# A fused attention and two-MoE kernel whose order of work comes from a planner: new DMA and TensorE costs in the planner, another gate and rank for the first W_out, early scales for the second weights, and half-size store buffers

## The chip, the cores and the metric

One Trainium2 chip, one core. The metric is the device time of one execution in microseconds (us), as the median over runs. The engines are named as in the profile: PE is TensorE's matmul side and PEld its weight loads, DVE is VectorE, ACT is ScalarE, POOL is GpSimd, and SP is SyncE, whose queue issues nearly all DMAs here.

## The reference, cut to what matters

Causal attention with a linear memory branch, mixed by a per-head gate, feeds two feed-forward layers with different activations, one after the other, on 2304 tokens.

```python
B, H, S, D = (4, 8, 576, 64)
scores = scale * np.matmul(q, k.transpose(0, 1, 3, 2))      # causal mask, softmax -> a
local = np.matmul(a, v)
mem_out = einsum(phi(q), M_prev) / (einsum(phi(q), z_prev) + 1e-06)
x = g * mem_out + (1 - g) * local                           # -> (2304, 512)
h = x @ w_in;  x = (h * sigmoid(h)) @ w_out                 # layer 0: 512 -> 2048 -> 512
h = x @ w_in2; y = (h * tanh(softplus(h))) @ w_out2         # layer 1: the same sizes
```

## The kernel before, in words

**Order of the work.** The kernel text does not issue instructions in the order in which it stands. Each operation is handed to a `Plan` (line 58 on) with a priority, the regions that it reads and writes, its engine or choice of engines, and a cost in ns. `Plan.issue` (line 105) then plays the whole program through as a list scheduler: at each step the engine that is free first takes, among the operations that are ready by then, the one with the smallest priority number, and that fixes each engine's in-order instruction stream. An operation is ready when what it depends on has ended plus a latency `LAT` (by the engine that produced it, `LAT["SP"]` for anything that comes by DMA) plus `MORE` for some pairs of engines. A DMA ends at `max(moved, issue end + 650) + tail`, so that the planner's DMAs pass one after the other; `tail` is bytes/360 for a copy (line 416) and 112 ns for each 128x128 block of a transpose (line 594). A priority decides only between operations that are ready together: an engine with nothing better takes whatever is there, and does not break it off. On the chip each stream runs in order, so an instruction that is planned too early makes everything behind it on its engine wait.

**Stages.** Attention goes in 80 steps (16 head pairs x query blocks, two visits each; `stage_a` line 538: scores, mask, exponentials, split into two f16 parts, a DMA transpose; `stage_b`: probabilities x values and normalisation, three steps later; `stage_c`: a PE transpose into x). Its results go by DMA into `xd`, and layer 0 takes them in 9 chunks of 256 tokens. Chunk 0 needs steps 0 to 7, chunk 1 (the second chunk) steps 8 to 15, and so on. For a chunk, `chunk_x` (line 775) scales x and splits it into two f16 parts, `gemm1` computes one of 8 groups of hidden columns in 24 matmuls of 128x256 (three products of parts), `hidden` applies the activation, and `gemm2` adds 24 matmuls more into the output banks. The buffers of the hidden values are 7 deep. `flush` copies a chunk's outputs into two staging buffers `w` and stores them to `yd`. Layer 1 uses 7 products of quarter blocks in place of 8 (`gemm1`, `gemm2` with l = 1) and reads its weights in that form.

**First weights.** `weights_of(k)` (line 955) handles W_in (k = 0, units 0 to 7) and W_out (k = 1, units 8 to 15), 1 MB each. A unit is loaded (`ws<-w` or `w<-w` in the profile), turned from float64 bits into float32 by two ACT operations and one on DVE (`single`: ACT L705, ACT L348, DVE L356), and its products with itself (8 matmuls `banks<-w` into `gram`) give a bound from which `weight_scale` finds one scale for all 8 units. Only then `weight_split` makes the two f16 parts of each (an ACT copy and a DVE operation). The load of unit u waits for the single of unit u - FLIGHT, and W_out's loads wait also for the split of attention step GATE (line 1023). `W_PRIO` (line 911) gives W_in's work the priority -2e5 + u and W_out's -1e5 + u; the attention steps below 8 have -1.5e5 + 2.3 n and the others 2.3 n. Work of the MoE on ACT, DVE and POOL has -1e6 + i and so goes first; its matmuls have 1e6 + i and so go last.

**Second weights.** `weight_single` (line 737) loads each of the 16 units of layer 1 during attention, makes it single, notes its largest square sum (`squares`, into `topw`) and stores it to `wd`. When chunk 8's input is set up, `weight_scale(1, k)` finds the two scales from `topw` (`largest`, line 659: a DVE product with the identity, a small matmul `banks<-diag,onesf` into bank 7, a DVE maximum), and `weight_pair` (line 757) loads the units again, forms sums of blocks and writes two f16 parts of 1792 columns. Units 0 to 7 go into the space that attention has left, 8 to 11 into that of the first weights when these are done with, and 12 to 15 (u >= LATE) through one buffer, the second stage `wb[1]`, into `wp` in HBM, from where `weight_fetch` brings them back.

Of the kernel before, what the change touches and what calls it, by code (L numbers as in the profile page):

```python
# [41 lines left out]
G_AHEAD = 3  # L42
G_DEEP = 7
LEAD = 7
GATE = 4
FLIGHT = 4
LATE = NU - NU // 4


# [9 lines left out]
class Plan:  # L59

    LAT = {"PE": 197, "ACT": 250, "DVE": 220, "POOL": 130, "SP": 920}
    MORE = {("ACT", "POOL"): 20, ("DVE", "POOL"): 20, ("POOL", "PE"): 45, ("PE", "ACT"): 17}

    def __init__(self):
# [120 lines left out]
def attn_moe_moe2_kernel(ctx: ExitStack, tc: tile.TileContext, kq, vm, beta, w1, w2, out):  # L187
# [88 lines left out]
    def carve(shape, dt, n=1):  # L276
        ts = []
        for _ in range(n):
# [9 lines left out]
            if len(shape) > 1:  # L288
# [27 lines left out]
    b8r = ring([wb[0], wb[1], side[0], side[1], wb[0], wb[1], side[0], wb[0],  # L316
                side[0], wb[0], side[0], wb[0], side[0], wb[0], wb[1], side[0]])
    tw = w_first[:, 2048 * NU + 2048:2048 * NU + 4096].bitcast(F32)
    w_out2 = w_first[:, 0:NU // 2 * 3584].rearrange("p (u s b c) -> p u s b c", u=NU // 2, s=2, b=7)


# [54 lines left out]
    def stt(prio, out, in0, s, in1, op0, op1):  # L376
        plan.add(prio, [c_stt(out, in0, s, in1, op0, op1)], [out], aps(in0, s, in1), shared=not ps(in0) and not ps(in1))
# [17 lines left out]

    def mm(prio, ms, whole=False):

        ns, edge, before = 0, None, 0
        for o, l, r, _, _ in ms:
            n = cols(o)  # L400
            load, one, times = (107, 2 * n / 2.4 + 2.5, 2) if r.dtype == F32 else (107 if r.dtype == F32R else 14, n / 2.4 + 2.5, 1)
            for _ in range(times):
                ns += (one + (0 if edge is None else max(0, load - before))) * l.shape[0] / 128
                edge = (edge or (load, 0))[0], one
                before = one

        def go():
            for o, l, r, a, z in ms:
                nc.tensor.matmul(out=o, lhsT=l, rhs=r, start=a, stop=z)  # L409

        writes = [m[0] for m in ms]
        if whole:
            writes = [(t, 0, 128, b0 // 2048 * 2048, -(-b1 // 2048) * 2048) for t, _, _, b0, b1 in map(plan.region, writes)]
        plan.add(prio, [("PE", ns, go)], writes, [x for m in ms for x in m[1:3]], edge=edge)

    def dma(prio, out, in_, writes=None, reads=None):
        nbytes = 128 * cols(out) * SIZE[out.dtype]
        plan.add(
            prio, [("SP", 475, lambda: nc.sync.dma_start(out=out, in_=in_))],
            [out] if writes is None else writes, [in_] if reads is None else reads, tail=nbytes / 360)  # L420

    def other(prio, e, ns, fn, writes, reads=()):
        plan.add(prio, [(e, ns, fn)], writes, reads)
# [114 lines left out]
    def stage_a(n, sbk, prio):  # L538

        v, qt = STEPS[n]  # L540
        nk = qt + 1
        N = min(S, 128 * nk)
        b0 = 512 * sbk[turn[0] % len(sbk)]
        turn[0] += 1
        ph, P, m1 = phr(), pr(), mr()
        if qt < 4:

            scs = [banks[:, b0 + 512 * e:b0 + 512 * e + N] for e in range(2)]
            ms, nb = [], 4 * nk
            for e, sc in enumerate(scs):  # L550
                r, c = slice(64 * e, 64 * e + 64), slice(128 * (qt % 2), 128 * (qt % 2) + 128)
                if qt < 2:
                    ms.append([(sc, qq[v, 0][r, c], rk[v][r, 0:N], True, False)])
                else:
                    kh, kl, (qh, ql) = *kk[v], qq[v, 1]
                    ms.append([(sc, qh[r, c], kh[r, 0:N], True, False), (sc, qh[r, c], kl[r, 0:N], False, False),
                               (sc, ql[r, c], kh[r, 0:N], False, False)])
            masks = [(sc[:, N - 128:N], ident16, mask[:, 0:128], False, True) for sc in scs]
            mm(prio, [x for y in zip(*ms) for x in y] + masks)
            both = banks[:, b0:b0 + 1024].rearrange("p (e c) -> p e c", e=2)[:, :, 0:N]  # L560
            P = P[:, 0:2 * N].rearrange("p (e c) -> p e c", e=2)
            ph_ = ph[:, 0:nb].rearrange("p (s e k) c -> p s e (k c)", s=2, e=2)
            tiles = [(P[:, e], scs[e], m1[:, e:e + 1]) for e in range(2)]
        else:
            nb = 2 * nk
            both = banks[:, b0:b0 + N]
            kh, kl = kk[v]
            hi, lo = [t.rearrange("p e q -> p (e q)") for t in q4s]
            ms = []
            for a, z in ((0, 512), (512, N)):  # L570
                ms += [(both[:, a:z], hi, kh[:, a:z], True, False), (both[:, a:z], hi, kl[:, a:z], False, False),
                       (both[:, a:z], lo, kh[:, a:z], False, z < N)]
            mm(prio, ms + [(both[:, N - 64:N], ident16, mask[:, 128:192], False, True)])
            pad = P[:, N:128 * nk]
            other(prio, "POOL", 90, lambda: nc.gpsimd.memset(pad, 0.0), [pad])
            tiles = [(P[:, 0:N], both, m1[:, 0:1])]
            P = P[:, 0:128 * nk]
            ph_ = ph[:, 0:nb].rearrange("p (s k) c -> p s (k c)", s=2)
        m1 = m1[:, 0:len(tiles)]
        other(prio, "DVE", 1.04 * cols(both) + 70, lambda: nc.vector.tensor_reduce(  # L580
            out=m1, in_=both, axis=AX, op=ALU.max, negate=True), [m1], [both])
        for o, sc, m in tiles:
            act(prio, o, sc, AF.Exp, 1.0, m)
        copy(prio + D_S, ph_[:, 0], P, PSCALE)
        stt(prio + D_S, ph_[:, 1], P, PSCALE, ph_[:, 0], ALU.mult, ALU.subtract)
        plan.mark(f"step{n}")
        ph = ph[:, 0:nb]

        live = pt_live[1 - LAG:]
        p0 = next(x for x in [pt_live[-1][1], 0] + [z for _, z in live] if x + nb <= PT_BLOCKS and all(  # L590
            z <= x or x + nb <= a for a, z in live))
        pt_live.append((p0, p0 + nb))
        pt = pts[n] = pt_tile[:, p0:p0 + nb, :]
        plan.add(prio, [("SP", max(1180, 400 + 113 * nb), lambda: nc.sync.dma_start_transpose(
            out=pt, in_=ph.rearrange("p n c -> p (n c)")))], [pt], [ph], tail=112 * nb)

    def last(n):
        v, qt = STEPS[n]
# [36 lines left out]
    def stage_c(n, prio):  # L635

        if not last(n):
            return
        v, qt = STEPS[n]
        p = VISITS[v][0]  # L640
        x, R = xts.pop(n)
        m = 1 + qt % 2
        for i in range(m):
            x2, o = x[:, i].rearrange("p e d -> p (e d)"), bank[6 + i][:, 260:260 + R]
            plan.add(prio, [("PE", 56, lambda o=o, x2=x2: nc.tensor.transpose(o, x2, ident[0:R, 0:R]))], [o], [x2, ident],  # L645
                     edge=(107, 56))
        b, hp = divmod(p, H // 2)
        if b == 0 and qt < 2:
            copy(prio, xs0[:, hp].rearrange("p (b c) -> p b c", b=m),
                 banks[:, 512 * 6:512 * 8].rearrange("p (b c) -> p b c", b=2)[:, 0:m, 260:260 + R])  # L650
            return
        xo = xor_()[:, 0:m * R]
        copy(prio, xo.rearrange("p (b c) -> p b c", b=m),
             banks[:, 512 * 6:512 * 8].rearrange("p (b c) -> p b c", b=2)[:, 0:m, 260:260 + R])
        t0, n = column(b, 256 * (qt // 2)), m * R
        dma(prio, xd[128 * hp:128 * hp + 128, t0:t0 + n], xo, writes=[("xd", hp, hp + 1, t0, t0 + n)])
# [100 lines left out]
    def weight_pair(u, prio):  # L757
# [4 lines left out]
                            ("POOL", "DVE"))  # L762
        sc, v = wsc[1][:, k:k + 1], b8[:, 256:2048]
        d = (w_in2, w_out2)[k][:, j].rearrange("p s b c -> p s (b c)")
        w = wb[1].bitcast(F16)[:, 0:3584].rearrange("p (s n) -> p s n", s=2) if u >= LATE else d
        act(prio, w[:, 0], v, AF.Copy, sc)
        stt(prio, w[:, 1], v, sc, w[:, 0], ALU.mult, ALU.subtract)
        if u >= LATE:
            dma(prio, wp[u - LATE], wb[1].bitcast(F16)[:, 0:3584], writes=[("wp", u, u + 1, 0, 1)])

    def weight_fetch(u, prio):
        dma(prio, w_first[:, 3584 * (u - NU // 2):3584 * (u - NU // 2 + 1)], wp[u - LATE], reads=[("wp", u, u + 1, 0, 1)])


    def chunk_x(l, c, prio, spot):
# [132 lines left out]
    D_B, D_C, D_Q, D_K, D_P, D_V, D_S = 2.5, 3.2, 4.0, 4.0, 3.0, 6.0, 0.5  # L908
    A_RATE, MOE_B, L_V = 2.3, -1e6, 0.0
    att_prio = lambda n, d=0: A_RATE * (n + d) + (ATT_B if n < N0 else 0)  # L910
    MOE, W_PRIO, ATT_B = MOE_B, (-2e5, -1e5), -1.5e5

    def prep(v, prio):
        if VISITS[v][1][-1] >= 2:
# [66 lines left out]
    def inputs(l, c, prio):  # L981

        nonlocal n_att
        if l == 0:
# [4 lines left out]
                n_att += 1  # L989
            for u in range(NU * (c - 1) // TOPS, min(NU, NU * c // TOPS)) if c else ():  # L990
                weight_single(u, att_prio(12 + 3.5 * u))
        xs_of[l, c] = chunk_x(l, c, prio, bank[0] if (l, c) == (0, 0) else bank[7])
        if (l, c) == (0, NT // TOK - 1):
            for k in range(2):
                weight_scale(1, k, 1e5 + NU, bank[7])
            for u in (*range(NU // 2), *range(LATE, NU)):
                weight_pair(u, 1e5 + NU + u)

# [83 lines left out]
```

## Time and profile before

| | us |
|---|---|
| median of 3 runs (966.07 to 967.75) | 966.64 |
| the profiled execution | 968.1 |
| its span, first to last instruction | 966.2 |
| mean granted TensorE clock | 0.973 |
| PE busy in the span | 911.2 (94%) |
| DVE, ACT, POOL busy | 725.1, 609.4, 404.9 |
| time in which the 16 DMA engines' packets of the SP queue were moving | 51.0% |

PE's busy time is that of overlapping matmuls; what it was not busy for are gaps in which its next matmul waited for something. The granted clock is the share of TensorE's full 2.4 GHz that was granted: 0.5 is 1.2 GHz.

### The profile page before, as it was taken

What the parts mean: (1) busy time and instruction counts of PE and PEld (TensorE: products, weight loads), DVE (VectorE), ACT (ScalarE), POOL (GpSimd) and SP (SyncE); (2) the same over time, 40 slices, a digit from 0 to 9 for tenths busy, and PEclk for the clock granted to TensorE, in tenths of its full rate; (3) what the DMA queues carried; (4) which work ended last, traced back from release to release, by engine and by line L of the source; (5) the groups of instructions that cost most, each with busy time, mean ns of one, the idle gap of its engine ahead of it and who ended that gap; (6) DMA issues with size and microseconds to landing.
All of it is one profiled execution on the core that took longest, in us unless ns stands there. A gap on an engine that the chain in (4) does not pass through costs nothing.

```text
span 966.2 us, 25452 instructions
## 1 busy us (share of the span) xinstructions
PE 911.2 (94%) x10436; PEld 800.8 (83%) x10436; DVE 725.1 (75%) x1534; ACT 609.4 (63%) x1074; POOL 404.9 (42%) x573
## 2 busy tenths in 40 slices
PE   4659989899999989999998999999999999999997
PEld 3547878787878878788887888999999999999996
DVE  5797877697778878778458735757887888878775
ACT  7897888787878866666345545544645545544543
POOL 1113223233324525334334767454545635635453
PEclk9658999999999999999999999999999999999999
DMA  9987399899899896866422433320010010010010
GB/s 283 333 293 190 68 300 272 206 284 224 219 280 244 213 197 161 172 139 117 97 90 88 148 121 127 127 93 24 23 46 23 24 45 24 24 43 14 13 24 22
DMA packets 154579, 131.28 MB, mean 136 GB/s; under 512 B 111712, under 2 KB 138848, under 8 KB 150368
## 3 DMA queue, kind: packets, MB, share of 16 engines
q1 hardware_dynamic: 154320, 129.68, 51.0%
q8 instruction: 81, 1.33, 0.6%
q14 instruction: 34, 0.28, 0.1%
q10 hardware_dynamic: 144, 0.00, 0.0%
HBM read 77.75 MB, written 25.69 MB: 107 GB/s over the span
## 4 chain that ended last, share of the span: by engine, by line
PE 78%; DMA 9%; DVE 6%; ACT 4%; issue 2%; SPq 0%; POOL 0%; DVEq 0%; ACTq 0%
PE banks L409 77%; DMA arena<-vm 2%; ACT arena L348 2%; DVE w L356 1%; DMA arena<-kq 1%; DMA wp<-ws 1%; DMA w<-w 1%; DMA yd<-w 1%; PE banks L645 1%; DVE arena L356 1%; ACT w L348 1%; DVE ws L356 1%; ACT ws L348 1%; DMA ws<-w 1%; DVE arena L362 1%
## 5 line engine op out<-in xcount | busy, mean ns | idle before, releaser
L409 PEld LDWEIGHTS <-w 128*128 128x128 f16 (+1 forms) x3584 | 346.5, 100 | 68.0 <-DVE w L356 19.6
L409 PE MATMUL banks<-arena 128*128 128x128 f16 (+6 forms) x4752 | 295.6, 223 | 19.0 <-ACT arena L348 8.0
L409 PEld LDWEIGHTS <-arena 128*128 128x128 f16 (+1 forms) x4464 | 232.4, 100 | 20.6 <-issue 11.3
L409 PE MATMUL banks<-xh,w 128*128 128x256 f16 x1728 | 211.7, 273 | 4.3 <-DVE ga L356 3.3
L409 PE MATMUL banks<-g,w 128*128 128x256 f16 x1728 | 211.2, 274 | 2.2 <-ACT w L348 2.1
L409 PE MATMUL banks<-w,g 128*128 128x256 f16 x1512 | 181.1, 273 | 0.0
L409 PEld LDWEIGHTS <-g 128*128 128x128 f16 x1512 | 144.1, 98 | 15.1
L362 POOL TENSOR_TENSOR g<-ga,g 128x512 f16<-128x512 f32 x71 | 96.8, 1366 | 110.5 <-ACT g L348 105.0
L362 POOL TENSOR_TENSOR arena<-arena 128x256 f32<-128x256 f32 (+1 forms) x71 | 60.1, 852 | 125.8 <-DVE arena L362 110.5
L356 DVE SCALAR_TENSOR_TENSOR arena<-arena 128x256 f16<-128x256 f32 (+6 forms) x144 | 106.6, 748 | 7.6 <-ACT arena L348 7.4
L362 POOL TENSOR_TENSOR xh<-xh 128x128 f32<-128x128 f32 x139 | 70.9, 533 | 92.5 <-ACT xh L348 90.5
L348 ACT ACTIVATE arena<-arena 128x256 f32<-128x256 f32 (+6 forms) x179 | 101.1, 591 | 9.3 <-PE banks L409 5.2
L362 POOL TENSOR_TENSOR w<-w 128x128 f32<-128x128 f32 x140 | 79.7, 592 | 45.6 <-ACT w L348 43.5
L348 ACT ACTIVATE arena<-banks,arena 128x128 f32<-128x128 f32 (+4 forms) x144 | 73.8, 545 | 32.2 <-DVE arena L580 29.3
L356 DVE SCALAR_TENSOR_TENSOR ga<-ga,banks 128x512 f32<-128x512 f32 x72 | 49.1, 683 | 41.0 <-ACT ga L348 40.4
L348 ACT ACTIVATE ga<-banks,xsc 128x512 f32<-128x512 f32 x72 | 49.1, 684 | 40.9 <-PE banks L409 39.2
L580 DVE TENSOR_REDUCE arena<-banks 128x2 f32<-128x256 f32 (+3 forms) x80 | 64.1, 802 | 11.9 <-PE banks L409 10.1
L356 DVE SCALAR_TENSOR_TENSOR g<-w,xsc,g 128x384 f16<-128x384 f32 (+1 forms) x72 | 55.6, 776 | 15.6 <-ACT g L348 15.6
L356 DVE SCALAR_TENSOR_TENSOR g<-xh,xsc,g 128x384 f16<-128x384 f32 (+1 forms) x72 | 54.5, 759 | 15.6 <-ACT g L348 13.3
L348 ACT ACTIVATE w<-banks 128x128 f32<-128x128 f32 x72 | 19.5, 270 | 67.9 <-PE banks L409 67.9
L348 ACT ACTIVATE g<-w,xsc 128x384 f16<-128x384 f32 (+1 forms) x72 | 47.0, 660 | 19.2 <-POOL w L362 18.9
L348 ACT ACTIVATE g<-xh,xsc 128x384 f16<-128x384 f32 (+1 forms) x72 | 47.6, 663 | 16.5 <-POOL xh L362 15.0
(118 smaller groups left out, 1129.6 us busy)
## 6 DMA issues: line engine op xcount, KB each, us to landing
ws<-w SPq DMA_DIRECT2D x22, 1024.0 KB, 6.7
arena<-kq SPq DMA_DIRECT2D x16, 576.0 KB, 5.1
w<-w SPq DMA_DIRECT2D x8, 1024.0 KB, 9.4
wd<-w SPq DMA_DIRECT2D x16, 512.0 KB, 4.6
arena<-vm SPq DMA_DIRECT2D x16, 325.0 KB, 3.6
yd<-w SPq DMA_DIRECT2D x36, 128.0 KB, 2.7
ws<-wd SPq DMA_DIRECT2D x9, 512.0 KB, 3.5
xs<-yd SPq DMA_DIRECT2D x9, 512.0 KB, 3.7
```

The costliest lines, as they stand in the source:

```text
L348: return ("ACT", ns, lambda: nc.scalar.activation(out=out, in_=in_, func=func, scale=scale, bias=bias))
L356: return ("DVE", 1.04 * cols(out) + 160 - over[0], lambda: nc.vector.scalar_tensor_tensor(out=out, in0=in0, scalar=s, in1=in1, op0=op0, op ...
L362: return (e, ns, lambda: eng.tensor_tensor(out=out, in0=in0, in1=in1, op=op))
L409: nc.tensor.matmul(out=o, lhsT=l, rhs=r, start=a, stop=z)
L580: other(prio, "DVE", 1.04 * cols(both) + 70, lambda: nc.vector.tensor_reduce(out=m1, in_=both, axis=AX, op=ALU.max, negate=True), [m1], [b ...
L645: plan.add(prio, [("PE", 56, lambda o=o, x2=x2: nc.tensor.transpose(o, x2, ident[0:R, 0:R]))], [o], [x2, ident], edge=(107, 56))
```

## The change

- In the planner: `LAT["SP"]` from 920 to 1800 ns; a copy's tail from bytes/360 to bytes/315; a transpose's tail from 112 to 220 ns a block; f32 and f32r matmuls and the PE transposes of `stage_c` get other costs (the f16 matmuls keep theirs).
- GATE from 4 to 2 and FLIGHT from 4 to 3.
- W_out's priority from -1e5 + u to 20 + u, so 28 to 35; attention step 8 has 18.4, step 12 has 27.6 and step 15 has 34.5.
- `weight_scale(1, k)` is called right after the last single of each half of the second weights, with the priority -1e6, and no longer at chunk 8's input with 1e5 + 16.
- Units 12 to 15 of the second weights: three rotating buffers of one part each (`tw`, and the two halves of `wb[1]`) and two stores of 448 KB, where there was one buffer of both parts and one store of 896 KB.

```diff
-GATE = 4
-FLIGHT = 4
+GATE = 2
+FLIGHT = 3
-    LAT = {"PE": 197, "ACT": 250, "DVE": 220, "POOL": 130, "SP": 920}
+    LAT = {"PE": 197, "ACT": 250, "DVE": 220, "POOL": 130, "SP": 1800}
+    halfr = ring([tw.bitcast(F16)[:, 0:1792], *[wb[1].bitcast(F16)[:, 1792 * i:1792 * i + 1792] for i in range(2)]])
-        ns, edge, before = 0, None, 0
+        ns, edge = 0, None
         for o, l, r, _, _ in ms:
             n = cols(o)
-            load, one, times = (107, 2 * n / 2.4 + 2.5, 2) if r.dtype == F32 else (107 if r.dtype == F32R else 14, n / 2.4 + 2.5, 1)
-            for _ in range(times):
-                ns += (one + (0 if edge is None else max(0, load - before))) * l.shape[0] / 128
-                edge = (edge or (load, 0))[0], one
-                before = one
+            load, more = (107, 58) if r.dtype == F32 else (107, 42) if r.dtype == F32R else (14, 2.5)
+            one = max((2 if r.dtype == F32 else 1) * n / 2.4 * l.shape[0] / 128 + more, 30)
+            ns += one
+            edge = (edge or (load, 0))[0], one
-            [out] if writes is None else writes, [in_] if reads is None else reads, tail=nbytes / 360)
+            [out] if writes is None else writes, [in_] if reads is None else reads, tail=nbytes / 315)
-            out=pt, in_=ph.rearrange("p n c -> p (n c)")))], [pt], [ph], tail=112 * nb)
+            out=pt, in_=ph.rearrange("p n c -> p (n c)")))], [pt], [ph], tail=220 * nb)
-            plan.add(prio, [("PE", 56, lambda o=o, x2=x2: nc.tensor.transpose(o, x2, ident[0:R, 0:R]))], [o], [x2, ident],
+            plan.add(prio, [("PE", 131, lambda o=o, x2=x2: nc.tensor.transpose(o, x2, ident[0:R, 0:R]))], [o], [x2, ident],
-        w = wb[1].bitcast(F16)[:, 0:3584].rearrange("p (s n) -> p s n", s=2) if u >= LATE else d
-        act(prio, w[:, 0], v, AF.Copy, sc)
-        stt(prio, w[:, 1], v, sc, w[:, 0], ALU.mult, ALU.subtract)
+        w = [halfr() for _ in range(2)] if u >= LATE else [d[:, i] for i in range(2)]
+        act(prio, w[0], v, AF.Copy, sc)
+        stt(prio, w[1], v, sc, w[0], ALU.mult, ALU.subtract)
         if u >= LATE:
-            dma(prio, wp[u - LATE], wb[1].bitcast(F16)[:, 0:3584], writes=[("wp", u, u + 1, 0, 1)])
+            for i in range(2):
+                dma(prio, wp[u - LATE, :, 1792 * i:1792 * i + 1792], w[i], writes=[("wp", u, u + 1, i, i + 1)])
-    MOE, W_PRIO, ATT_B = MOE_B, (-2e5, -1e5), -1.5e5
+    MOE, W_PRIO, ATT_B = MOE_B, (-2e5, 20.0), -1.5e5
                 weight_single(u, att_prio(12 + 3.5 * u))
+                if u % (NU // 2) == NU // 2 - 1:
+                    weight_scale(1, u // (NU // 2), MOE, bank[7])
         if (l, c) == (0, NT // TOK - 1):
-            for k in range(2):
-                weight_scale(1, k, 1e5 + NU, bank[7])
```

## Rows read from the trace of the kernel before

**Rows 1.** Busy time by stage; after each engine's us the instructions, then clock, DMA share, GB/s.

```profile
0.00:34.00 34.00, 18.93 (x124) 12.95 (x124) 21.00 (x52) 25.63 (x48) 4.76 (x27) 0.99 0.97 312
34.00:77.36 43.36, 27.03 (x203) 20.88 (x204) 37.05 (x79) 38.48 (x59) 5.17 (x6) 0.50 0.99 295
77.36:515.00 437.64, 420.28 (x4576) 351.50 (x4575) 335.91 (x693) 316.64 (x578) 154.96 (x169) 1.00 0.80 191
515.00:966.20 451.20, 444.95 (x5537) 415.43 (x5535) 331.11 (x712) 228.62 (x391) 239.98 (x371) 1.00 0.17 54
```

**Rows 2.** Timeline of PE, around the first gemm1 and the first gemm2.

```profile
73.77 2.74 PE L409 MATMUL banks<-w 128*128 128x128 bf16 x24 [1.70 <-DVE w L356]
...
77.36 2.04 PE L409 MATMUL banks<-xh,w 128*128 128x256 f16 x15
...
99.89 0.49 PE L409 MATMUL banks<-g,w 128*128 128x256 f16 x3
...
101.07 8.02 PE L409 MATMUL banks<-g,w 128*128 128x256 f16 x72
```

**Rows 3.** Groups by line in 40 to 77.36 us: busy, mean ns, idle before.

```profile
L409 PE MATMUL banks<-w 128*128 128x128 bf16 x64 | 7.9, 309 | 6.9 <-DVE w L356 6.9
...
L705 ACT ACTIVATE w<-ws 128x1024 f32<-128x1024 f32 x4 | 4.5, 1133 | 2.5 <-DMA ws<-w 2.4
...
L705 ACT ACTIVATE w<-w 128x1024 f32<-128x1024 f32 x3 | 3.4, 1123 | 0.0
```

**Rows 4.** Timeline of DVE: the first and the last of three W_out singles.

```profile
57.18 1.22 DVE L356 SCALAR_TENSOR_TENSOR w<-w,ws 128x1024 uint32<-128x1024 uint32 x1
...
63.18 1.22 DVE L356 SCALAR_TENSOR_TENSOR w<-w 128x1024 uint32<-128x1024 uint32 x1
```

**Rows 5.** Timeline of ACT after the first gemm1: two waits, the last W_out single.

```profile
78.06 0.62 ACT L348 ACTIVATE arena<-banks,arena 128x128 f32<-128x128 f32 x2 [2.29 <-DVE arena L580]
...
81.65 0.38 ACT L348 ACTIVATE arena<-banks 128x256 f32<-128x256 f32 x1 [2.21 <-PE banks L645]
...
84.43 1.13 ACT L705 ACTIVATE w<-w 128x1024 f32<-128x1024 f32 x1
```

**Rows 6.** Timeline of SP's queue: the longest issue of a transpose.

```profile
24.51 8.43 SPq L594 DMA_TRANSPOSE arena<-arena  x1
```

**Rows 7.** DMA issues: count, KB each, median us from issue to landing.

```profile
ws<-w SPq DMA_DIRECT2D x22, 1024.0 KB, 6.7
...
yd<-w SPq DMA_DIRECT2D x36, 128.0 KB, 2.7
...
wp<-ws SPq DMA_DIRECT2D x4, 896.0 KB, 5.3
...
arena<-arena SPq DMA_TRANSPOSE x80, 5.0
```

**Rows 8.** Timeline of PE: the three gaps of over 2 us after 78 us.

```profile
220.39 0.81 PE L409 MATMUL banks<-g,w 128*128 128x256 f16 x6 [2.13 <-ACT w L348]
...
362.74 0.49 PE L409 MATMUL banks<-diag,onesf 128*128 128x128 f32 x2 [2.43 <-DVE arena L362]
...
514.64 2.01 PE L409 MATMUL banks<-xh,w 128*128 128x256 f16 x9 [2.71 <-DVE ga L356]
```

**Rows 9.** Busy time of the 20 us around each of these gaps, columns as in rows 1.

```profile
220.00:240.00 20.00, 19.53 (x208) 16.10 (x208) 14.72 (x36) 16.68 (x29) 6.19 (x8) 0.91 1.00 233
360.00:380.00 20.00, 17.52 (x185) 14.18 (x184) 17.14 (x37) 12.34 (x23) 10.51 (x12) 1.00 0.74 170
500.00:520.00 20.00, 16.89 (x139) 14.28 (x137) 17.32 (x32) 10.32 (x10) 9.03 (x6) 0.91 0.28 87
```

**Rows 10.** Chain that ended last: pieces ahead of the first two of these gaps.

```profile
213.59 5.79 DMA yd<-w
...
360.61 4.31 DMA yd<-w
```

**Rows 11.** Timeline of ACT: the first split of the second weights.

```profile
504.59 1.79 ACT L348 ACTIVATE arena<-ws,wsc 128x1792 f16<-128x1792 f32 x1 [4.82 <-DVE wsc L353]
```

More of the change, by code (lines that the diff above doesn't have):

```diff
@@ L764, in weight_pair @@
         d = (w_in2, w_out2)[k][:, j].rearrange("p s b c -> p s (b c)")
-        w = wb[1].bitcast(F16)[:, 0:3584].rearrange("p (s n) -> p s n", s=2) if u >= LATE else d
-        act(prio, w[:, 0], v, AF.Copy, sc)
-        stt(prio, w[:, 1], v, sc, w[:, 0], ALU.mult, ALU.subtract)
+        w = [halfr() for _ in range(2)] if u >= LATE else [d[:, i] for i in range(2)]
+        act(prio, w[0], v, AF.Copy, sc)
+        stt(prio, w[1], v, sc, w[0], ALU.mult, ALU.subtract)
         if u >= LATE:
-            dma(prio, wp[u - LATE], wb[1].bitcast(F16)[:, 0:3584], writes=[("wp", u, u + 1, 0, 1)])
+            for i in range(2):
+                dma(prio, wp[u - LATE, :, 1792 * i:1792 * i + 1792], w[i], writes=[("wp", u, u + 1, i, i + 1)])
     def weight_fetch(u, prio):
-        dma(prio, w_first[:, 3584 * (u - NU // 2):3584 * (u - NU // 2 + 1)], wp[u - LATE], reads=[("wp", u, u + 1, 0, 1)])
+        dma(prio, w_first[:, 3584 * (u - NU // 2):3584 * (u - NU // 2 + 1)], wp[u - LATE], reads=[("wp", u, u + 1, 0, 2)])
     def chunk_x(l, c, prio, spot):
```

## The prediction

> **What bounds the kernel now.** The first view is the busy time by stage [rows 1]. In the last stage, from 515 us on, PE is busy for 444.95 of 451.20 us, and what is missing is nearly all the end, where the last outputs are drained. Here PE is the bound and nothing of the change touches its matmuls. From 77.36 to 515 us it is busy for 420.28 of 437.64, so 17.4 us are gaps. Before 77.36 it is busy for 18.93 + 27.03 of 77.36 us: 31.4 us are gaps, and the 27.03 us of the second row ran at a granted clock of 0.50, the 1.2 GHz level. So at most some 49 us of gaps and 13.5 us of half clock are to be had, and three fifths of it lie before the first gemm1.
>
> The second view is the timeline of PE there [rows 2]. The first gemm1 begins at 77.36 us, right behind 24 W_out matmuls; the first gemm2 at 99.89, without a gap before it. From then on PE always has gemm work, so an earlier first gemm1 moves everything behind it, provided that W_out is ready when the hidden buffers are full. What holds gemm1 back is ACT and DVE, busy for 38.48 and 37.05 of 43.36 us [rows 1]. The groups by line [rows 3] tell with what: seven W_out singles stand on ACT in this stretch (4 + 3 operations of L705 of 1.13 us, each followed by a second one that I take at the same length), 7 x 2.26 = 15.8 us, though their result isn't needed before 99.89.
>
> The third view is PE's gaps one by one after 78 us [rows 8]. Three are over 2 us, 2.13 + 2.43 + 2.71 = 7.3 of the 17.4 us; the other 10.1 us are pieces below that. Around two of them the granted clock of 20 us is 0.91 in place of 1.00 [rows 9], that is 0.09 x 20 / 0.5 = 3.6 us at half clock, 1.8 us lost for each.
>
> **The change part by part.** The sum is made against the profiled execution, 968.1 us, of which 966.2 are the span and 1.9 lie around it; the median of the runs shown is 966.64, 1.5 lower, and the difference is carried over to it.
>
> *Step 1, W_out behind the second chunk's attention.* On the path to the first gemm1 W_out costs three things. ACT stood for 2.4 us in front of a W_out load that had not landed [rows 3], with W_in's and the attention's work queued behind it. On DVE three W_out singles of 1.2 us stand among the W_in splits and the normalisation of chunk 0's last step [rows 4], 3.6 us. And the 24 matmuls ahead of gemm1 took 2.74 us at half clock [rows 2]. Together 8.7 us, if all of it goes and nothing takes its place. But the planner fills a free engine with whatever is ready, and steps 8 to 11 now stand in W_out's place; their pieces are shorter, so that they hold up less. I take -5.0, between 0 and -8.7.
>
> *Step 2, what is late next: gemm2.* The singles taken off ACT there have to be made after it, in competition with `hidden` (which goes first) and steps 8 to 11. Before, PE had 22.5 us between first gemm1 and first gemm2: at 8.02/72 us a matmul [rows 2] a gemm1 of 24 is 2.7 us, eight for a chunk 21.4 us, and the rest attention. Eight can be worked off before the buffers are full. With gemm1 5 us earlier PE has work of its own until some 94 + 5 = 99 us. If W_out's last single, at 84.43 us [rows 5], moves little, this costs nothing; if all 15.8 us move behind gemm1, less the 4.5 us in which ACT now waits there [rows 5], gemm2 comes 11.3 us later, at 111, and PE stands for 12. The loads themselves aren't the limit, since GATE lets them begin two steps sooner. I take +2.5, between 0 and +14 (12 and one return to half clock of 1.8).
>
> *Step 3, three loads in flight, GATE 2.* The longest issue of a transpose took 8.43 us [rows 6], with four loads of 1 MB queued ahead of it; SP could issue nothing else, neither attention inputs nor the next load. With three queued the stall should be shorter by about one load's passage. Against it, the fourth load waits for the first single. Nothing shows the net: between -3 and +2.5; I take 0, as W_in's chain is bound by ACT and DVE after 40 us.
>
> *Step 4, the planner's costs.* Worked out for the mean transpose of 10 blocks, the old planner had 1.53 + 0.65 + 1.12 + 0.92 = 4.2 us from issue to landing and the new has 6.2; the trace shows 5.0 [rows 7]. For 128 KB it is 2.4 and 3.3 against 2.7; for 1 MB 5.0 and 6.3 against 6.7. So the old costs are short for all three and the new ones long for the first two. In an in-order queue the two errors don't cost the same: planned too early, the instruction makes all behind it wait; planned too late, other ready work goes first, and PE has some nearly always. The first two gaps of rows 8 stand behind stores to `yd` of 5.79 and 4.31 us in the chain [rows 10], twice and 1.6 times the median of 2.7 [rows 7]: a staging buffer was not free when the copy into it came up, and gemm2 waited for that copy. These two, 2.13 + 2.43 + 1.8 of clock = 6.4 us, should mostly go, and a part of the 10.1 us in pieces; but a new order brings gaps of its own. The f32 and transpose costs on PE change only when the planner thinks PE free; their matmuls are the same. I take -4.5, between -11 and +4.
>
> The Trainium skill (TensorE: Matmul & The Clock Gate, Part 1) says that the throttled clock is the default state and that activity releases it. The trace agrees around the gaps at 220 and 514 us (0.91), not at 362 us (1.00) nor in the first 34 us (0.99 with PE busy for little over half) [rows 1, 9]; by the rule the third gap would be worth 1.8 us more, -6.3 in place of -4.5.
>
> *Step 5, early scales and half buffers.* ACT waited 4.82 us for the scale and then began on splits of 1.79 us each [rows 11], and `hidden` waits for one that is under way; PE's gap of 2.71 us at 514.64 stands behind that [rows 8]. With the scale ready before chunk 8 the splits can begin some 5 us sooner and spread out: 2.7 + 1.8 of clock = 4.5 us at best. Against it, two more small `diag` matmuls stand among attention and wait on PE's queue for DVE; such a one waited 2.43 us [rows 8], with all of gemm and attention queued behind it, so up to +4.8. I take -2.0. The half buffers shorten a row of stores of 5.3 us each [rows 7] between which ACT and DVE wait for the one buffer; while it ran PE had gemm work of layer 0, so it is 0 now, and a cover only if PE comes there some 10 us earlier. Four more issues on SP and the shared `tw` cost nothing there for the same reason.
>
> Sum: -5.0 + 2.5 + 0 - 4.5 - 2.0 = -9.0, so 959.1 us in a profiled execution and **957.6 us** as a median.
>
> **The rivals.**
>
> *More comes than forecast.* Step 1 near its end (-8), gemm2 not late (0), SP's stalls shorter (-2), step 4 at -7, step 5 at -3: -20, 947 us. For it speaks that each end is a row; against it that work displaced from a full ACT has to go somewhere.
>
> *The priorities don't bite.* ACT and DVE have free moments before 77 us, a ready W_out single is taken whatever its number, and three singles on DVE were planned there although W_in's and chunk 0's work came first by priority even then. Then first gemm1 and gemm2 stay, and the reordering trades one gap for another: 966, within 2.
>
> *Slower: W_out comes too late.* All seven singles fall behind steps 8 to 12 and behind the first single of the second weights (27.6, so ahead of all of W_out; three ACT operations like L705's, 3.4 us). gemm2 then begins at 111 + 3 = 114 us against work until 99: PE stands for 15 and loses 1.8 to the clock. With -5 from step 1 and -6.5 from steps 4 and 5 that is +5.3, 972 us. It decides from where gemm2 comes more than some 11 us after PE has run dry. For it speaks that ACT is the fullest engine there; against it that ACT waited 4.5 us right after 77 us and that the same work as before is to be done by gemm2's start.
>
> **How the numbers follow.** The forecast has 0.50, more than forecast 0.20, no bite 0.10, too late 0.20. What a measurement of this kernel can tell from no change is about 0.2%, 1.9 us. Faster by more than that: the first two and little of the third, 0.72; within it 0.08; slower, the last, 0.20. The likeliest case alone lies between 951 and 964, by steps 1 and 2, of which one gives back what the other brings. Eight times in ten takes in the low rival's centre and the slower one's: 947 to 972 us.
>
> **What would show it.** In the profile after, the first gemm1 (`banks<-xh,w`) should come at 69 to 74 us and W_out's matmuls for the most part behind it; the first gemm2 (`banks<-g,w`) at 98 to 103 with a gap of at most 3 us. The transposes' issues on SP before 40 us should stay under 6 us. The three gaps over 2 us should be gone, and the stage from there to 515 us should have some 11 us of gaps, not 17.4. No wait of ACT for `wsc` should be left about 500 us, and from 520 us on the trace should read as before, earlier by the difference. A first gemm1 not earlier than 76 us, or a gap of 6 us and more before the first gemm2, makes the forecast wrong; so do new gaps of over 2 us between 100 and 500 us.

## The result, and the profile after

The changed kernel takes 953.01 us (median of 4 runs, 951.2 to 954.03) against 967.19 us of the kernel before in the same comparison: a ratio of 0.9848, 95% interval 0.9822 to 0.9874. That is 14 us faster where 9 were forecast, inside the range. The profiled execution took 952.23 us, its span is 950.1.

The first view is the busy time by stage, first of the kernel after with the stages of [rows 1].

```profile
0.00:34.00 34.00, 16.20 (x116) 10.61 (x116) 19.00 (x51) 25.29 (x48) 4.80 (x27) 0.96 0.94 267
34.00:77.36 43.36, 30.66 (x241) 23.15 (x242) 35.17 (x79) 35.18 (x60) 6.62 (x8) 0.64 0.86 247
77.36:515.00 437.64, 429.80 (x4688) 361.81 (x4687) 346.15 (x694) 329.42 (x585) 159.37 (x173) 0.99 0.81 198
515.00:950.10 435.10, 428.37 (x5395) 400.75 (x5393) 326.46 (x711) 226.50 (x385) 229.32 (x368) 1.00 0.17 57
```

The same view cut at 120 us tells more, since by then the wait for W_out is over in both kernels. After:

```profile
0.00:120.00 120.00, 85.89 (x742) 65.87 (x742) 91.53 (x206) 100.37 (x178) 26.38 (x48) 0.83 0.88 240
120.00:515.00 395.00, 390.78 (x4302) 329.69 (x4301) 308.79 (x617) 289.51 (x514) 144.41 (x159) 1.00 0.80 196
```

and before:

```profile
0.00:120.00 120.00, 88.61 (x752) 69.96 (x753) 94.65 (x206) 97.38 (x169) 23.00 (x46) 0.82 0.81 234
120.00:515.00 395.00, 377.64 (x4151) 315.36 (x4150) 299.31 (x617) 283.36 (x516) 141.89 (x156) 1.00 0.83 199
```

Up to 120 us the change wins nothing: PE is busy 2.7 us less at nearly the same clock. From 120 to 515 us its gaps fall from 17.4 to 4.2 us, and that is most of the 16.1 us by which the span is shorter.

One reading of [rows 1] has to be put right for the clock. The 0.99 of the first 34 us is not a measured level: the trace before has its first clock record at 30.05 us (after: at 24.13), and the view counts what has no record as 1.00. The matmuls show the other level there. Two sets of eight products of a weight unit, before:

```profile
15.38 1.04 PE L409 MATMUL banks<-w 128*128 128x128 bf16 x8 [4.70 <-DVE w L356]
31.38 0.63 PE L409 MATMUL banks<-w 128*128 128x128 bf16 x8
```

The first took as long as such sets at a recorded 0.50 (1.03 us at 62.05), the second as those at 1.00 (0.62 us at 89.97). So the time up to the first record is counted at 0.50 from here on, and a loss is PE's gaps plus half of the time that it was busy at 0.50. Over the whole span that is 55.0 + 25.7 = 80.7 us before and 45.1 + 20.0 = 65.0 after, 15.7 of the 16.1 us. Up to 120 us it is 53.7 and 54.1, from 120 to 515 us 19.2 and 4.2.

The start does look as drawn, and more so. The timeline of PE in the kernel after, around the first gemm1, the last W_out matmuls and the first gemm2, to be set beside [rows 2]:

```profile
64.08 0.37 PE L409 MATMUL banks<-xh,w 128*128 128x256 f16 x1 [1.59 <-ACT xh L349]
66.55 1.86 PE L409 MATMUL banks<-xh,w 128*128 128x256 f16 x8 [2.10 <-DVE xh L357]
...
95.33 3.44 PE L409 MATMUL banks<-xh,w 128*128 128x256 f16 x30
...
103.80 1.03 PE L409 MATMUL banks<-w 128*128 128x128 bf16 x8 [1.99 <-DVE w L357]
...
109.18 0.40 PE L409 MATMUL banks<-g,w 128*128 128x256 f16 x1
110.93 1.05 PE L409 MATMUL banks<-g,w 128*128 128x256 f16 x8 [1.36 <-DVE w L357]
```

The first gemm1 comes 13.3 us sooner, though PE waits again after its first matmul, until 66.55 us; the first gemm2 comes 9.3 us later. Chunk 0's gemm1s are used up at some 99 us, and for ten us PE has only attention and W_out's own products. W_out's last single, at 84.43 us before [rows 5], is on ACT at

```profile
99.45 1.14 ACT L705 ACTIVATE w<-w 128x1024 f32<-128x1024 f32 x1
```

Busy time, clock and DMA of the wait, and of the part of it at half clock:

```profile
100.00:112.00 12.00, 8.57 (x60) 5.71 (x58) 10.07 (x28) 10.04 (x21) 2.93 (x3) 0.72 1.11 228
102.64:109.46 6.82, 5.64 (x37) 3.84 (x37) 5.73 (x21) 4.90 (x12) 0.00 (x0) 0.50 1.16 281
```

3.4 us of gaps, and 5.64 us of work at half clock, which is 2.8 us more lost: together some 6 us. That is about what the early gemm1 and the clock had won by then (up to 95 us the loss is 47.6 us, before 53.7). From chunk 1's first gemm2, at 148.7 us as against 148.4 before (counted off in the trace, 192 matmuls to a chunk), both kernels stand level with their gemms; by chunk 4's the changed one is 26 us ahead (336.8, 363.2), more than all the loss of the middle, so a part of it is attention put off; at layer 1's first gemm2 it is 16.3 (617.6, 633.9).

What PE waited for from 120 to 515 us, after:

```profile
PE banks L409 <- POOL g L363: 0.9, 1, 0.9
PE banks L645 <- DVE mx L366: 0.9, 1, 0.9
```

and before:

```profile
PE banks L409 <- DVE arena L362: 5.6, 6, 2.4
PE banks L409 <- ACT arena L348: 3.4, 3, 1.6
PE banks L409 <- DVE ga L356: 3.1, 2, 2.7
PE banks L409 <- ACT w L348: 2.1, 1, 2.1
```

All three gaps of [rows 8] are gone and no group of waits is over 1 us. That is the middle; which part of the change emptied it is for the experiments.

### The profile page after: what moved, and what is told of

Read it like the earlier page. It is cut to its first block, busy times and chain, and to the rows that moved or that the text cites. A ratio compares the mean times of both kernels' runs of the same rounds, so it can differ in the third digit from the quotient of the medians.

```text
span 950.1 us, 25452 instructions
## 1 busy us (share of the span) xinstructions
PE 905.0 (95%) x10436; PEld 796.3 (84%) x10436; DVE 726.8 (76%) x1532; ACT 616.4 (65%) x1075; POOL 400.1 (42%) x574
## 4 chain that ended last, share of the span: by engine, by line
PE 55%; DVE 1%; ACT 1%; issue 1%; DMA 0%; POOL 0%; ACTq 0%; DVEq 0%
PE banks L409 55%; DVE arena L357 0%; ACT arena L349 0%; PE banks L645 0%; DVE ws L357 0%; ACT w L349 0%; DVE arena L363 0%; DMA yd<-w 0%; POOL g L363 0%; DVE diag L354 0%; DVE mx L366 0%; ACT g L349 0%; ACT ga L349 0%; DVE ga L357 0%; DVE w L357 0%
## 5 line engine op out<-in xcount | busy, mean ns | idle before, releaser
L357 DVE SCALAR_TENSOR_TENSOR arena<-arena 128x256 f16<-128x256 f32 (+6 forms) x144 | 112.5, 789 | 11.2 <-ACT arena L349 11.0
L363 POOL TENSOR_TENSOR arena<-arena 128x256 f32<-128x256 f32 x72 | 64.8, 907 | 132.7 <-DVE arena L363 113.1
L349 ACT ACTIVATE arena<-arena 128x256 f32<-128x256 f32 (+6 forms) x184 | 105.0, 593 | 20.6 <-PE banks L409 15.8
L349 ACT ACTIVATE arena<-banks,arena 128x128 f32<-128x128 f32 (+4 forms) x144 | 73.7, 546 | 32.0 <-DVE arena L580 23.8
L357 DVE SCALAR_TENSOR_TENSOR g<-w,xsc,g 128x384 f16<-128x384 f32 (+1 forms) x72 | 54.9, 770 | 17.2 <-ACT g L349 16.8
L349 ACT ACTIVATE g<-ga 128x512 f16<-128x512 f32 x72 | 45.2, 628 | 18.6 <-DVE ga L357 18.2
```

Of the source, the lines that this page charges most:

```text
L349: return ("ACT", ns, lambda: nc.scalar.activation(out=out, in_=in_, func=func, scale=scale, bias=bias))
L357: return ("DVE", 1.04 * cols(out) + 160 - over[0], lambda: nc.vector.scalar_tensor_tensor(out=out, in0=in0, scalar=s, in1=in1, op0=op0, op ...
L363: return (e, ns, lambda: eng.tensor_tensor(out=out, in0=in0, in1=in1, op=op))
```

## The experiments

All stand against the kernel before on the same chip (its medians were 972.1, 969.6 and 970.6 us in the three sets), so ratios are compared. "Costs" is LAT["SP"], the DMA tails and the f32 and transpose costs; "rank" is W_out's priority with GATE 2 and FLIGHT 3; "scales" the early scales and the half buffers. The gaps are 395 less PE's busy time from 120 to 515 us, in the one profiled execution of each kernel. The theories' times were written for 967.2 us before; a ratio of 0.99 is 957.5 us on that scale.

**Set 1: one part at a time.** Costs alone (`e1_costs`):

```diff
-    LAT = {..., "SP": 920}
+    LAT = {..., "SP": 1800}
-    tail=nbytes / 360    tail=112 * nb
+    tail=nbytes / 315    tail=220 * nb
```

with the diff's lines for f32 matmuls and `stage_c`'s transposes.

> The kernel before with the planner's new costs alone (LAT, DMA tails, f32 and transpose costs); W_out's rank, GATE, FLIGHT, scales and half buffers stay old. Theory A, the costs carry the gain: the stage from 120 to 515 us loses little, some 953 to 956 us. Theory B, the rank of W_out with GATE and FLIGHT carries it, since attention is ahead afterwards: 965 us or more. Theory C, the early scales carry a third (the gap at 514 us): about 958 us with a gap of over 2 us at chunk 8.

Measured: 0.992 (0.9892 to 0.9947), 964.1 us (959.5 on that scale, between the theories). The middle did become calmer (7.1 us of gaps, of which 4.8 from 130 to 160 us), but the second weights took 6.2 us back, and up to 120 us the loss is 55.3 us as against 53.7. Busy time of both stretches:

```profile
130.00:160.00 30.00, 25.21 (x231) 19.89 (x230) 21.94 (x52) 23.36 (x45) 7.44 (x9) 0.94 0.99 264
515.00:640.00 125.00, 118.79 (x1208) 107.24 (x1206) 83.74 (x124) 68.56 (x89) 85.15 (x80) 1.00 0.42 136
```

Rank alone (`e2_rank`):

```diff
-GATE = 4, FLIGHT = 4, W_PRIO = (-2e5, -1e5)
+GATE = 2, FLIGHT = 3, W_PRIO = (-2e5, 20.0)
```

> The kernel before with W_out's new priority, GATE 2 and FLIGHT 3 alone. Theory A: gemm1 starts earlier, gemm2 later, and the middle keeps its 17 us of gaps: 965 to 970 us. Theory B: 955 to 958 us.

Measured: 0.9839 (0.9806 to 0.9872), 955.9 us, as much as the whole change, with 6.2 us of gaps in the middle. Theory A, which I had from the two traces, had this wrong. The start came out better than in the whole change: first gemm1 at 63.4, first gemm2 at 103.1 us, and a loss up to 120 us of 49.9 us as against 53.7 before and 54.1 after.

Scales and half buffers alone (`e3_scales`): only the diff's lines for the half buffers (`halfr`) and for `weight_scale`.

> The kernel before with the early scales and the half buffers alone. Theory A: the gap of 2.7 us near 514 us and its half clock go, 962 us. Theory C: 960 us or less. If the gap only moves: 966 us.

Measured: 0.9923 (0.9892 to 0.9954), by time theory C's. But the middle has 14.9 us of gaps, some of them in new places.

The whole without the rank (`e4_old_rank`):

```diff
-GATE = 2, FLIGHT = 3, W_PRIO = (-2e5, 20.0)
+GATE = 4, FLIGHT = 4, W_PRIO = (-2e5, -1e5)
```

> The changed kernel with W_out's old priority, GATE 4 and FLIGHT 4. Theory A: 951 to 953 us, because the 7 us that PE loses between 100 and 112 us, waiting for W_out, come back against the 5 us by which gemm1 then starts later. Theory B: 962 us or more.

Measured: 0.9855 (0.9822 to 0.9887), 957.6 us, 7.3 us of gaps. The wait between 100 and 112 us is gone (PE is busy for all 12 us), but gemm1 comes at 76.8 us, and the loss up to 120 us is 54.7 us, no less than with the wait. So the rank alone, the rest without it, and both together come out alike. Parts that add up to 3% by themselves and to 1.5% together may remove the same thing, or each of them may merely deal out a new order. The next set asks that.

**Set 2: what is chance, what is cover.** A LAT without a meaning of its own, to see how far any new order moves the time (`h5_before_lat_900` from the kernel before, `h4_lat_1700` from the changed one):

```diff
-    LAT = {..., "SP": 920}
+    LAT = {..., "SP": 900}
```

> The kernel before with 900 in place of 920 in LAT, the same question for the order of before. Theory D: the middle from 120 to 515 us loses 10 us or less in place of 21, and the time is 960 us or less. Theories A and F: 964 to 970 us, with the middle still losing 15 us or more.

Measured: 0.9901 (0.9875 to 0.9926), 959.9 us; 7.9 us of gaps in place of 17.4, as theory D had it. Twenty ns in a planner's constant are worth 9.7 us (969.6 to 959.9).

> The changed kernel with 1700 in place of 1800 in LAT, a difference without a meaning of its own, for how far any new order moves the time. Theory D (chance of the order): off by 4 us or more from the changed kernel. Theories A and F: within 2 us.

Measured: 0.9881 (0.9837 to 0.9926), 5.6 us of gaps. Its interval holds the changed kernel's 0.9848, so a difference isn't shown.

Old DMA times in the changed kernel (`h2_old_dma`: LAT and both tails back).

> The changed kernel with LAT and both DMA tails of before, so with the rank, the scales and the f32 costs. Theory A (the DMA times calm the middle): 958 to 962 us, with stalls of PE behind transposes and stores again. Theory F (rank and costs remove the same stalls, either alone is enough): 952 to 956 us.

Measured: 0.9875 (0.9827 to 0.9922), 957.9 us; 10.0 us of gaps. By time (955.1 on the theories' scale) that is theory F's, but PE does wait for transposes again, as theory A had it:

```profile
PE banks L409 <- DMA arena<-arena: 3.8, 4, 1.3
```

That holds for all the runs. In each of the seven with the old DMA times (before, 940, 900, e3, e2, k2 and this one) PE waits for a DMA from 120 to 515 us, by 0.8 to 4.5 us in all; in none of the seven with the new ones (after, e1, e4, h1, h4, k3, k4) does it.

Late scales and the one buffer in the changed kernel (`h1_no_scales`: the lines for half buffers and `weight_scale` back).

> The changed kernel with the late scales and the one store buffer of before. Theory E (covered cost): PE now reaches the second weights' splits about 16 us sooner, so that their late start is no longer hidden; the stretch from 515 to 640 us loses some 5 us, as in the run with the costs alone: 957 to 959 us against 952 to 953 of the changed kernel. If scales and buffers are worth what they brought to the kernel before alone: 960 us.

Measured: 0.9907 (0.9877 to 0.9938), the middle at 2.6 us of gaps. The stretch in which the second weights are made, busy time and then PE's two long gaps in it:

```profile
515.00:640.00 125.00, 118.81 (x1203) 107.09 (x1201) 84.91 (x126) 69.61 (x90) 77.96 (x79) 0.99 0.42 138
```

```profile
625.56 3.12 PE L408 MATMUL banks<-w,g 128*128 128x256 f16 x27 [1.65 <-ACT w L348]
633.64 1.38 PE L408 MATMUL banks<-arena 128*128 128x128 f16 x12 [2.61 <-DVE w L362]
```

Here 6.2 us are missing; in the changed kernel it is 0.6:

```profile
515.00:640.00 125.00, 124.37 (x1326) 113.36 (x1325) 83.37 (x128) 67.81 (x96) 73.35 (x87) 1.00 0.39 132
```

The kernel before missed next to nothing there with the same late scales (124.83 of 125 us busy), and its PE came later: chunk 8's first gemm2 is at 598.7 us there, at 589.6 here and at 582.5 in the changed kernel. `e1_costs` shows the same loss, 6.2 us, with PE there at 593.0. So theory E's number came true, but its reason is at most a part of it. In `e2_rank` PE comes there at 585.2 us, sooner than here, with the same late scales, and misses only 2.4 us (`k2_rank_lat_900`: 588.2 and 2.4). What sets this run and `e1_costs` apart from those two is that under the new costs the splits themselves begin later. The first one, here and in `e2_rank`, beside 504.59 us in the kernel before [rows 11]:

```profile
522.97 1.79 ACT L348 ACTIVATE arena<-ws,wsc 128x1792 f16<-128x1792 f32 x1 [5.80 <-DVE wsc L353]
```

```profile
505.96 1.78 ACT L348 ACTIVATE arena<-ws,wsc 128x1792 f16<-128x1792 f32 x1
```

In `e1_costs` it is at 524.4 us, in the changed kernel, with the early scales, at 485.9. Why the late scale comes 18 us later under the new costs was not taken apart.

**Set 3: more orders of each kind, and an attempt to have the wait for W_out back.**

940 in LAT of the kernel before (`k1_before_lat_940`):

> The kernel before with 940 in place of 920 in LAT: a third order from the old costs and the old rank. PE's gaps from 120 to 515 us were 17.4 us in the kernel before and 7.9 with 900. Theory D (the order of before was an unlucky one, and the old costs give 8 us as a rule): 6 to 10 us of gaps, 957 to 961 us. Theory F (old costs and old rank give long gaps as a rule, 900 was lucky): 13 us or more, 965 us or more.

Measured: 0.9899 (0.9842 to 0.9957), by time theory D's; 12.0 us of gaps, between the theories.

The rank alone with 900 in LAT (`k2_rank_lat_900`):

> The kernel before with the rank of W_out, GATE 2, FLIGHT 3 and 900 in LAT: a second order from the old costs with the new rank, where the first had 6.2 us of gaps from 120 to 515 us and came out 1.6% faster. Theory F: again 6 to 10 us of gaps and a ratio of 0.983 to 0.990. Theory D: anything from 6 to 17 us, ratio up to 1.00.

Measured: 0.9876 (0.9838 to 0.9914), in theory F's range; 11.0 us of gaps, above it.

The whole without the rank, with 1700 in LAT (`k4_old_rank_1700`):

> New costs, early scales and half buffers with the old rank, GATE 4 and FLIGHT 4, and 1700 in LAT: a second order from the new costs with the old rank (the first had 7.3 us of gaps from 120 to 515 us and came out 1.45% faster). Theory F: 5 to 9 us of gaps, ratio 0.983 to 0.988. Theory D: 3 to 15 us.

Measured: 0.984 (0.9804 to 0.9876); 5.9 us of gaps, both in theory F's range.

W_out's rank at 10 in the changed kernel (`k3_rank_10`):

```diff
-    W_PRIO = (-2e5, 20.0)
+    W_PRIO = (-2e5, 10.0)
```

> The changed kernel with 10 in place of 20 for W_out's priority, so 18 to 25, level with steps 8 to 11 and ahead of step 12. If the wait for W_out between 100 and 112 us can be had back without losing the early first gemm1: gemm1 at 64 to 70, gemm2 at 101 to 105 us, no gap of over 1 us before it, and 947 to 951 us, faster than the changed kernel. If earlier W_out singles again hold up gemm1 by as much: 953 to 957 us.

Measured: 0.9897 (0.9861 to 0.9933), 961.5 us. The first gemm2 does come at 101.5 us (the first gemm1 at 66.5), but now PE waits for the second chunk's attention. Busy time from 130 to 160 us and in the part of it at half clock, first here, then the whole in the changed kernel:

```profile
130.00:160.00 30.00, 22.62 (x186) 17.33 (x185) 19.15 (x51) 21.15 (x42) 5.57 (x9) 0.77 1.03 235
137.13:150.78 13.65, 9.34 (x50) 6.17 (x51) 10.37 (x29) 9.50 (x20) 0.93 (x3) 0.50 0.98 275
```

```profile
130.00:160.00 30.00, 30.00 (x307) 25.37 (x305) 20.43 (x51) 24.86 (x51) 6.36 (x9) 1.00 1.03 240
```

7.4 us of gaps and 9.34 / 2 = 4.7 us of clock. So that is what the rank of 20 buys with the 6 us before 112 us: chunk 1's attention in time. The old rank under the new costs shows the same, smaller (4.8 us of gaps there in `e1_costs` and `e4_old_rank`).

All orders by kind, gaps from 120 to 515 us and ratio (`k3_rank_10`, with a third rank, is left out):

| costs | rank | gaps, us (ratio) | mean gaps | mean loss up to 120 us | mean ratio |
|---|---|---|---|---|---|
| old | old | before 17.4 (1), 940: 12.0 (0.990), with scales 14.9 (0.992), 900: 7.9 (0.990) | 13.0 | 52.6 | 0.993 |
| old | new | k2 11.0 (0.988), h2 10.0 (0.988), e2 6.2 (0.984) | 9.1 | 50.7 | 0.986 |
| new | old | e4 7.3 (0.986), e1 7.1 (0.992), k4 5.9 (0.984) | 6.8 | 55.7 | 0.987 |
| new | new | h4 5.6 (0.988), after 4.2 (0.985), h1 2.6 (0.991) | 4.1 | 54.9 | 0.988 |

A letter and number stand for the run that begins so (e2 for `e2_rank`); the mean ratio of the first row is 0.991 without the kernel before. The rows aren't pure: h2 has the new f32 and transpose costs and the early scales, e1 and h1 have the late scales.

What follows: in the middle the new costs halve the gaps at either rank (13.0 to 6.8, 9.1 to 4.1) and scatter less (2.6 to 7.3 as against 6.2 to 17.4); the rank takes off some 3 to 4 us at either costs. The times do not follow the gaps. Up to 120 us the orders with the new costs lose 3 to 4 us more, and with late scales some 6 us at the second weights; by ratio the rank alone, the costs with the old rank and both come out alike (0.986 to 0.988). On top lies the luck of the one order that happened to be the kernel before: two neighbours of no meaning are 1% faster, two thirds of the 1.5%. Against these neighbours the changed kernel is ahead by about 0.5% and its own neighbour with 1700 by 0.2%, at intervals of 0.3 to 0.6% each way. No version beats the changed kernel beyond its interval; e2 and k4 stand level with it.

## Why the prediction was right, and where it was not

Sign and range held, in part by luck: the middle won far more than its term, one reason being that the kernel before was a slow order, and that made up for step 2. In losses the terms came to +0.4 up to 120 us (steps 1 to 3, forecast at -2.5), some -12 for step 4 (-4.5) and -4.4 for step 5 (-2.0).

*What bounds the kernel* left out a part of the half clock: the first 30 us ran at 0.50 too, as shown above, so the half clock before the first gemm1 cost 22 us and not 13.5. That the start spoke against the rule that the prediction cites falls with it.

*Step 1* (-5.0, at best -8.7) was too small as to the first gemm1, which moved by 13.3 us (its second matmul by 11). The best case wasn't one. [rows 4] has three of W_out's singles on DVE, 3.6 us; the trace before has seven ahead of the first gemm1 (the others at 45.86, 66.57, 70.10 and 72.49 us), and six of them went, 7.3 us. It also left out what each delay made late in turn: the maximum over chunk 0's x, on DVE, began at 57.8 us in place of 67.7. How that splits among the delays was not taken apart. That W_out's matmuls go behind gemm1 was right: seven of eight sets.

*Step 2* (+2.5, between 0 and +14) is the step that failed. W_out's last single moved from 84.43 to 99.45 us, gemm2 came 9.3 us later, near the 11.3 of its bad end, and the wait cost 3.4 us of gaps and 2.8 of half clock. PE was out of gemm work at 99 us, as worked out, but by luck: that sum had gemm1 begin at 72 us. The third rival's mechanism happened in the main, only that attention filled a part of the wait. The loads did not begin sooner either: W_out's first goes out at 37.1 us (36.0 before), and the last, which waits for the single three units back, at 87.3 (73.7). Up to 120 us steps 1 and 2 were forecast at -2.5, and with step 3 they came to +0.4 (53.7 to 54.1).

The rank by itself was forecast better: in `e2_rank` and `k2_rank_lat_900` gemm2 comes at 103.1 and 103.0 us, the end of the forecast's 98 to 103, and the start wins 3.8 and 4.9 us. What the sum lacked is that other parts of the change delay the start as well. In all four orders that have the new rank and the new f32 and transpose costs (after, h1, h2, h4) gemm2 comes at 108.5 to 110.9, in h2 with the old DMA times, in h1 with the late scales. Step 4 had put these f32 costs at nothing; they were not tried alone.

*Step 3* was set at 0 between -3 and +2.5, and the size was off. The longest issue of a transpose before 40 us fell from 8.43 to 6.10 us (I had said under 6), but the fourth load waits for the first single and for SP. The timeline of SP in the kernel after shows the issue that then held it:

```profile
11.88 6.10 SPq L594 DMA_TRANSPOSE arena<-arena  x1
```

The fourth W_in load goes out at 20.0 us, not 6.1, and the last one lands at 43.3 us in place of 36.4 (36.9 in `k4_old_rank_1700`, which has four in flight). Whether four in flight with the new rank would start gemm1 sooner still was not tried, nor GATE by itself.

*Step 4* (-4.5, between -11 and +4) had the mechanism in the middle, and not the size. The first two gaps of [rows 8] went, and so did nearly all pieces: 17.4 to 4.2 us of gaps, of which 2.7 belong to step 5. The loss there fell from 19.2 to 4.2 us; less these 2.7 it is some -12, past its good end. But only the first of them stood behind a store to `yd`. The second ended at 362.74 us, while the store of [rows 10] was under way until 364.92; what DVE had waited for just before was the next chunk's input:

```profile
361.14 1.22 DVE L365 TENSOR_REDUCE mx<-xs 128x1 f32<-128x1024 f32 x1 [2.34 <-DMA xs<-xd]
```

By the table the costs account for some 5 to 6 us of the gaps, the rank for 3 to 4, and the rest is that the kernel before had drawn a bad order, for which the sum had no term. That DMAs planned too early make PE wait is borne out by the seven runs against seven: no wait for a DMA is left with the new times. That it is the DMA times and not the f32 costs that halve the gaps rests on `h2_old_dma` alone (10.0 us of gaps with the f32 costs in place), one order. What the sum did not have at all is that the costs take 3 to 4 us back before 120 us.

*Step 5* (-2.0, between -4.5 and +4.8) was right in kind and small in size (-4.4: the gap of 2.7 us and 1.7 of clock). ACT no longer waits for `wsc` after 120 us, the gap at 514 us is gone, and the clock from 500 to 520 us is 1.00 in place of 0.91. The half of it that was costed at nothing, with the condition that PE come there 10 us sooner, is what happened: PE came 16 us sooner, and the one run without the scales and buffers (`h1_no_scales`) loses 6.2 us there, in part because its splits begin 18 us later. Which of the two edits carries it was not tried.

Of the rivals, "the priorities don't bite" fell (rank alone: 0.984), and so did "slower": its wait came in part (6 us lost, not 17) and was outweighed elsewhere. "More comes than forecast" is near by its time (947) but not by its terms, as it had gemm2 not late. The last stage, as said, reads as before, earlier by the difference.

## What to carry to other kernels

A long in-order schedule made by a greedy planner is one draw among many: change a constant by 2% first and see how far the time moves, and judge an edit by several such neighbours on either side, not by one pair. Making the planner's times for late things (DMA landings) a little too long took all waits for DMAs out of the middle here and brought the draws closer together there; judge it by the whole time all the same, for it cost enough elsewhere to do no better than a rank tuned by hand. And after an edit, look at what is next along the path: a preparation that was hidden before, as the second weights were, can be the bound afterwards, because the work reaches it sooner or because it begins later itself.

## What the runs showed that I had not expected

Gaps of PE brought half clock with them where they came one after the other: in the wait for W_out 3.4 us of gaps came with 2.8 us lost at half clock, in `k3_rank_10` 7.4 us with 4.7. Of the gaps of two to three us that stood alone in [rows 8] two did so too (0.91 in [rows 9]), and the one at 362 us did not (1.00).

Parts of a change that were each worth 0.8 to 1.6% alone gave 1.5% together. That fits each of them replacing the same unlucky order, but the runs do not prove that this is the reason.
